# A two-layer spectral and dense kernel: input rows in three parts, three stores from another queue, statistics and residual sums spread

## The chip, the cores and the metric

The kernel runs on one core of one Trainium2 chip. The metric is the device time of one execution in microseconds (us). Before the change it is 927.1 us, the median of three runs (926.85, 927.1 and 933.89). The profiled execution took 925.04 us; its span, from the first to the last instruction, is 923.2 us, with a granted TensorE clock of 1.000. Times with a position, such as 498.55, are us from the start of that span.

## What is computed

`x` is 2048 tokens by 1024 features in bfloat16. A spectral layer and a dense layer alternate twice, each behind a layer norm and with a residual sum:

```python
def _A_ref(x, w_r, w_i):
    X = rfft2(x.astype(f32))                 # 2048 x 513 complex
    return irfft2(X * (w_r + 1j * w_i), s=(S, D)).astype(bf16)
def _B_ref(x, w1, b1, w2):                   # F = 3584
    h = x @ w1 + b1
    return (h * tanh(softplus(h))) @ w2      # Mish
x = x + _A_ref(_layernorm(x)); x = x + _B_ref(_layernorm(x))
x = x + _A_ref(_layernorm(x)); x = x + _B_ref(_layernorm(x))
```

Both layers use the same weights both times. `_layernorm` has no gain and no offset: subtract the row's mean, divide by the root of its variance plus 1e-5.

## The kernel before

All five engines run programs that are written out once, in order. The Python code emits instructions to five lists (`Prog`); a helper (`op`, `group`, `dma`) adds the semaphore waits which the buffers need. So the order on each engine is the order in which the Python code emits, and an instruction that waits holds everything behind it on its engine. The 16 tiles of `x` (128 tokens each) stay in on-chip memory as `XS`; a second copy, `XR`, has the rows laid out for the transforms.

**Spectral layer (`layer_A`).** The two-dimensional transform is a chain of matrix products with tables.
- `s1` (L634): 16 groups j of 8 small matmuls read `XR`. Their results leave PSUM through ScalarE (L640) or VectorE (L642). In the first layer the table `M0` is multiplied by the reciprocal deviation of the rows first (`scaled`, L609 on ScalarE, L615 on VectorE and GpSimd), one 8-block for each j. Three pairs of PSUM banks go round in the first layer, four in the second.
- In the first layer `prologue` loads `XS` and then `XR` from HBM, all on SyncE's queue (L251 is the line of every DMA); `XR` in 24 DMAs of 256-byte rows, for j 0 to 7, 8 to 11 and 12 to 15. A group waits for the whole part that holds it.
- Then, for 8 groups g of frequencies, five kinds of steps, called by digits "stage, g, half": 2 is `s2` (L741), 3 is `s3` (L786 to L789) with the product with the filter on VectorE (L800 to L807), 4 is `i1` (L842), 5 is `i2` (L872, L904). `order_A` is the order of them, written out by hand and used in both layers. Each step takes the next of four PSUM pairs. An `i1` step waits for the filter product of the same g and half. In the first layer `filter_bins` (L1032, with copies on VectorE, L1043, and on ScalarE, L1047) sorts the filter's bins after `s2` of each g.
- The result goes to HBM and back transposed; the last transform (`i4`, L1071) and its exits from PSUM (L573 on ScalarE, L577 on VectorE) run in the dense layer. `spin` and `hold` (L651, L656, L1060) are matmuls with no use but to keep TensorE busy.

**Dense layer (`layer_B`).** Tokens in four chunks c of 512.
- *Opening*: `mm1` (L1220) computes the first hidden features with plain products, in 256-token halves at first, each followed by a Mish on ScalarE (L1224). Three PSUM banks go round, so the matmuls of one group wait for the Mish of the third before. While it runs, the tiles 4 to 7 get their residual sum (`residual`, L1498, VectorE), their statistics, and are normalised (`apply`, L522).
- Statistics of a tile are made by VectorE (`stats_dve`, L470) or by ScalarE (`stats_act`, L451: two passes over the tile, Copy for the sum and Square for the sum of squares). `sums_to_mv` (L462 to L464) and `scales` (L500 to L513), 11 small VectorE operations, turn the sums into a scale.
- *`quads`* (L1260): the other hidden features as 2 by 2 blocks with seven products instead of eight. In each step n VectorE adds partial results from PSUM (L1265), ScalarE applies Mish (L1270) and copies (L573). `after(n)` hangs other work on the step: statistics, residual sums of tiles 12 to 15, `apply`, loads. A product with `A22` reuses a PSUM bank that an L1265 addition must have read.
- *`products`* (L1359): the second matrix product, again with seven block products in place of eight; additions on VectorE (L1398, L1402, L1410).
- At the end of the first dense layer the finished tiles are normalised and stored to `xn_scratch` in HBM (`xn_store`, on GpSimd's queue), and SyncE loads them back as `XR` for the second spectral layer (`xr_load`). The last tile, 11, goes directly from on-chip memory (`xr_direct`, on three queues), while 31 matmuls of `spin` run.

Of the kernel before, what the change touches and what calls it, by code (L numbers as in the profile page):

```python
# [5 lines left out]
ACT = mybir.ActivationFunctionType  # L6
ALU = mybir.AluOpType
P = 128
# [172 lines left out]
class KB:  # L181
# [200 lines left out]
    def prologue(self):  # L382
        sp = self.sp
        self.op(self.pool, lambda e: e.memset(self.EPS[:], 1e-5), writes=[self.r_eps, self.r_warm])
        xt = self.x[0].rearrange("(t p) d -> p t d", p=P)

        for a, b in ((10, 11), (0, 1), (1, 2), (11, 12), (2, 3), (3, 4), (12, 13), (4, 6), (13, 14), (6, 8), (14, 15), (8, 10), (15, 16)):
            self.dma(self.act if a == 10 else sp, self.XS[:, a:b, :], xt[:, a:b, :], f"x{a}", writes=self.r_xs[a:b])
        self.warm(ACT.Sqrt)
        small = {}  # L390
        def load_small(name, n, d):
            b = self.alloc(name, self.o[name], [n], d)
            self.dma(sp, b.ap, self.con[name], name.lower(), writes=[b.res])
            small[name] = b
        load_small("M0", P, BF)
        load_small("IDF", P, F32)
        self.M0, self.IDF = small["M0"], small["IDF"]

        self.XR = self.alloc("XR", self.o["XR"], [P, P])
        self.r_xr = []  # L400
        xv = self.x[0].rearrange("(n2 n1) (h l) -> h n2 n1 l", n2=16, l=P)
        for q, n in ((0, 2), (2, 1), (3, 1)):
            r = Res(f"xr{q}")
            for h in range(8):
                s = slice(32 * q, 32 * (q + n))
                self.dma(sp, self.XR.ap[h:P:8, s, :], xv[h][:, s, :], f"xr{q}", parts=[r])
            self.r_xr += [r] * n
        self.dma(sp, self.FD[:], self.con["FD"], "fd", writes=[self.r_fd])
        load_small("JT", 4 * P, BF)
        self.JT, self.r_jt = small["JT"].ap, small["JT"].res  # L410
        self.w1_next = 0
# [31 lines left out]
                writes=rr)  # L443
        self.op(self.dve, lambda e: e.reciprocal(r, a), writes=rr)

    def stats_act(self, j):
        act = self.act
        x, sums, rs, junk = self.XS[:, j, :], self.BN[:, j, 0:2], self.r_mv[j], self.junk
        rs.begin()
        for i, f in enumerate((ACT.Copy, ACT.Square)):  # L450
            self.op(act, lambda e, i=i, f=f: e.activation(junk.ap, x, f, accum_out=sums[:, i:i + 1]),  # L451
                    reads=[self.r_xs[j]], writes=[junk.res], parts=[rs])

# [70 lines left out]
        return b  # L524


    def xn_store(self, j, b):
        b.unread = False
        self.dma(self.pool, self.xn_d[j].rearrange("h n l -> n h l"), b.ap.rearrange("n (h l) -> n h l", l=P), f"xw{b.res.name[2:]}",
                 reads=[b.res], writes=[self.r_xnd[j]])  # L530

    def open_xr(self):
# [86 lines left out]
    def s1(self, li):  # L619
        self.Y = self.alloc("Y", self.o["Y"], [P, P])  # L620
        self.Y.res.begin()
        M, XR = self.M, self.XR
        for j in range(4 if not li else 0):
            self.scaled(j)
        for j in range(16):
            if not li and self.npair % 4 == 3:

                self.npair += 1
            ps, banks, _ = self.pair()
            fns = []  # L630
            for q in range(8):
                n = 8 * j + q
                m = M[:] if li else self.MN.ap[:, n, :]
                fns.append(lambda e, q=q, n=n, ps=ps, m=m: e.matmul(ps[:, q * P:(q + 1) * P], XR.ap[:, n, :], m,  # L634
                                                                   start=True, stop=True))
            self.group(fns, reads=[self.r_xr[j // 4], self.r_m if li else self.r_mn[j]], writes=banks)
            src = ps.rearrange("p (q k) -> p k q", q=8)
            dst = self.Y.ap[:, :, 8 * j:8 * j + 8]
            if (j % 2 or j == 8) if li else j not in (5, 10, 14):
                self.op(self.act, lambda e, dst=dst, src=src: e.activation(dst, src, ACT.Copy), reads=banks, parts=[self.Y.res])  # L640
            else:
                self.op(self.dve, lambda e, dst=dst, src=src: e.tensor_copy(dst, src), reads=banks, parts=[self.Y.res])  # L642
            if not li and j + 4 < 16:
                self.scaled(j + 4)
        for r in ([self.MN.res, self.M0.res] + self.r_xr if not li else []):
            r.r(self.pe, self.pe.count)
            self.XR.res.r(self.pe, self.pe.count)
# [357 lines left out]
    @staticmethod  # L1005
    def order_A():


        order = ("200 201 210 211 300 301 220 310 400 221 311 401 230 320 410 500 231 321 411 501 330 331 420 510 240 511 421 241 "
                 "250 251 340 341 520 350 430 260 521 431 440 261 351 441 530 531 360 361 270 450 451 271 540 541 550 551 460 370 "  # L1010
                 "461 371 560 561 470 471 570 571")
        return [tuple(map(int, w)) for w in order.split()]
# [144 lines left out]
    def layer_B(self, li, last):  # L1157
        pe, dve, act, sp, pool = self.pe, self.dve, self.act, self.sp, self.pool
# [342 lines left out]
        def turns(c, *ts):  # L1501
            return [lambda t=t: transposed(c, t, xn[4 * c + t]) for t in ts]
# [50 lines left out]
            xn[j] = self.apply(j)  # L1553
        for fg in range(1, 4):
            mm1(0, fg, 1)
            if fg < 3:
                self.stats_act(5 + fg)
        if not last:
            mm1(0, 4)
        at_tiles(1)  # L1560
        B = {"B11": (XT[0].ap[:, 0:4, :], r_xt[0]), "B21": (XT[0].ap[:, 4:8, :], r_xt[0])}
        order = list(early)
        if last:
            block, corner, run = quads(list(range(4, 14)), order, B, [k * 1024 for k in (102, 140)])
            for n, bank in ((0, 3), (1, 4), (2, 5), (3, 0)):
                block(n, bank)
            corner(1, 4)
            turns(1, 0)[0]()
            corner(2, 5)
            turns(1, 1)[0]()  # L1570
            corner(3, 0)
        else:
            mm1(0, 5, mid=turns(1, 0, 1))
# [50 lines left out]
        def after(n):  # L1624
            again = {0: 7, 4: 8, 5: 9} if last else {0: 7}
            if n in again:
                self.fill_slot(order[again[n]], plain + again[n])
            if 1 <= n < 4:
                load_b(STD, n // 3, (n - 1) % 2)
            first = 6 if last else 4  # L1630
            if last:
                if n in (0, 2, 4, 5):
                    self.stats_act(8 + (0, 2, 4, 5).index(n))
                if n == 5:
                    self.xn_buf = self.xn_out + [self.alloc(f"XN{i}", self.ob["XN2"] + i * 2048, [self.D]) for i in range(2)]
                if n in (5, 7):
                    self.sums_to_mv(n + 3, 2)
                    self.scales(n + 3, 2)
            elif n < 4:
                self.stats_dve(8 + n)  # L1640
            elif n == 4:
                self.scales(8, 4)
            if n >= first:
                normal(8 + n - first)
                turn(4)
            for j in {first + 1: (12, 13), first + 2: (14,), first + 3: (15,)}.get(n, ()):
                residual(j)
        run(after, lead)
        self.junk = self.alloc("JUNK2", self.ob["JUNK2"], [self.D])
# [68 lines left out]
        order = [ws[n % 3] for n in range(14)]  # L1718
# [24 lines left out]
        def extra(n, t):  # L1743
            if last:
                return
            if (n, t) == (1, 0):
                PB[6][0] = load_w2("B21", 0, "Q3")
            if (n, t) == (2, 0):
                self.warm(ACT.Sqrt)
            if (n, t) == (3, 3):  # L1750
                self.open_xr()
                for j in range(8):
                    self.xr_load(j)
            if n == 5 and t < 3:
                self.xr_load(12 + t)
            if (n, t) == (5, 2):
                self.xr_load(15)
            if n in (4, 6):
                j = 4 * (n == 4) + 8 + t
                self.stats_second(j, 0, False)  # L1760
                self.root(j, 1)
                b = self.apply(j, out=True)
                if j == 11:
                    self.xr_direct(j, b, 2, (act, pool, sp, pool, sp, act, pool, sp))
                else:
                    self.xn_store(j, b)
            if n == 6 and t < 3:
                if t:
                    self.xr_load(7 + t)
            if (n, t) == (5, 3):  # L1770
                self.xr_load(10)
# [41 lines left out]
```

## Time and profile before

| us from start | stage | length | TensorE busy | VectorE busy | ScalarE busy |
|---|---|---|---|---|---|
| 24 to 42 | first `s1`, start of `s2` | 18 | 15.13 | 12.84 | 15.18 |
| 42 to 60 | first spectral layer, start | 18 | 17.04 | 17.73 | 17.42 |
| 60 to 104 | its rest | 44 | 41.92 | 35.71 | 37.33 |
| 104 to 170 | opening of the first dense layer | 66 | 62.21 | 40.51 | 37.65 |
| 170 to 304 | `quads`, first `products` | 134 | 134.00 | 109.50 | 50.97 |
| 304 to 474 | second half of that layer | 170 | 170.00 | 117.04 | 61.03 |
| 474 to 498 | tile 11, second `s1`, `s2` | 24 | 21.96 | 13.19 | 14.37 |
| 498 to 552 | second spectral layer | 54 | 51.38 | 41.93 | 46.04 |
| 552 to 610 | opening of the second dense layer | 58 | 54.38 | 34.96 | 36.78 |
| 610 to 669 | `quads` | 59 | 58.22 | 40.39 | 37.09 |
| 669 to 751 | `products` | 82 | 82.00 | 51.22 | 12.76 |
| 751 to 923 | second half of that layer | 172 | 168.96 | 91.01 | 50.45 |

Over the span TensorE is busy 877.7 us (95%), VectorE 623.4 (68%), ScalarE 435.0 (47%), GpSimd 147.7 (16%). A row of this table says what an engine did in that stretch, not whether anything waited for it. For that one reads the list of waits (which engine stood still, at which line, and whose instruction ended it), the chain (the path back from the last instruction, each piece with its start and length), and the timeline of one engine in a window, where `[0.62 <-ACT ...]` behind a row is the idle time ahead of it and what ended it. Rows of a timeline are: start, length, engine, line, operation, operands, how many in a row. The end that a matmul row shows lies after the time when the next could have started, because matmuls overlap: in a row of 40 with 256 columns (134.39, 4.53 us) they start about 0.109 us apart, and the last one's shown end is about 0.16 us after the next one's turn.

### The profile page before, as it was taken

How to read it: one execution, taken by the hardware profiler on the slowest of the kernel's cores; microseconds unless marked ns; L12 is line 12 of the kernel's file. 1: busy time of each engine (PE TensorE's matmuls, PEld its weight loads, DVE VectorE, ACT ScalarE, POOL GpSimd, SP SyncE). 2: the span in 40 equal slices, each digit the busy share in tenths (PEclk: the TensorE clock that was granted, in tenths of full speed). 3: DMA queues.
4: the chain of work that ended last, by engine and by line, in shares of the span. 5: the costliest groups of instructions: out<-in, count | busy, mean ns of one | idle time of the engine just before them, and what ended most of it. 6: DMA issues, size and time to landing. Idle time of an engine off the chain costs nothing.

```text
span 923.2 us, 13610 instructions
## 1 busy us (share of the span) xinstructions
PE 877.7 (95%) x5503; PEld 471.1 (51%) x5503; DVE 623.4 (68%) x995; ACT 435.0 (47%) x645; POOL 147.7 (16%) x170
## 2 busy tenths in 40 slices
PE   0899889999999999999998998999999999999998
PEld 0677576444444444444456766754444444444443
DVE  7798468686889667568767765676747655554463
ACT  7898485456203485420018966757540025552000
POOL 0732004960004651010121200000000000000000
PEclk9999999999999999999999999999999999999999
DMA  9979861575786388364723786345166645732432
GB/s 279 284 249 287 219 194 67 210 266 139 262 281 239 131 317 298 121 233 143 281 92 114 221 217 161 137 175 184 23 197 189 204 148 180 269 121 86 173 129 102
DMA packets 153502, 175.98 MB, mean 191 GB/s; under 512 B 75000, under 2 KB 132568, under 8 KB 153320
## 3 DMA queue, kind: packets, MB, share of 16 engines
q1 hardware_dynamic: 140256, 130.32, 45.9%
q0 software_dynamic: 10032, 42.90, 12.5%
q10 hardware_dynamic: 3152, 1.90, 0.7%
q8 instruction: 43, 0.70, 0.3%
q14 instruction: 19, 0.16, 0.0%
HBM read 130.78 MB, written 40.89 MB: 186 GB/s over the span
## 4 chain that ended last, share of the span: by engine, by line
PE 88%; DVE 6%; ACT 3%; SPq 2%; DMA 1%; issue 0%; DVEq 0%
PE PS L1359 37%; PE PS L1260 30%; PE PS L1220 6%; PE PS L741 3%; PE PS L842 2%; PE PS L872 2%; SPq L251 2%; PE PS L1071 2%; PE PS L634 1%; PE PS L651 1%; ACT ARENA L640 1%; PE PS L1181 1%; PE PS L904 1%; PE PS L1060 1%; ACT ARENA L451 1%; PE PS L656 1%
## 5 line engine op out<-in xcount | busy, mean ns | idle before, releaser
L1359 PE MATMUL PS<-ARENA 128*128 128x512 bf16 x1568 | 340.1, 379 | 0.0
L1260 PE MATMUL PS<-ARENA 128*128 128x512 bf16 (+1 forms) x1288 | 280.4, 379 | 0.8 <-DVE ARENA L1265 0.8
L1359 PEld LDWEIGHTS PS<-ARENA 128*128 128x128 bf16 x1568 | 153.3, 98 | 184.5
L1265 DVE TENSOR_TENSOR ARENA<-PS,ARENA 128x512 f32<-128x512 f32 x230 | 157.1, 691 | 100.2 <-PE PS L1260 92.4
L1260 PEld LDWEIGHTS PS<-ARENA 128*128 128x128 bf16 x1288 | 125.3, 98 | 153.3 <-DVE ARENA L1265 3.6
L1270 ACT ACTIVATE ARENA<-ARENA,B 128x512 bf16<-128x512 f32 x138 | 98.8, 721 | 69.1 <-DVE ARENA L1265 63.8
L573 ACT ACTIVATE ARENA<-PS 128x512 f32<-128x512 f32 (+3 forms) x86 | 61.6, 726 | 110.6 <-PE PS L1260 92.5
L1153 POOL TENSOR_TENSOR ARENA<-ARENA 128x512 bf16<-128x512 bf16 x56 | 71.5, 1278 | 74.3 <-DVE ARENA L522 61.1
L451 ACT ACTIVATE ARENA<-XS 128x1024 bf16<-128x1024 bf16 x60 | 63.2, 1053 | 36.6 <-DVE XS L1410 33.0
L1220 PE MATMUL PS<-ARENA 128*128 128x256 bf16 (+1 forms) x528 | 73.4, 295 | 3.4 <-DVE ARENA L1186 1.9
L1384 DVE TENSOR_TENSOR ARENA<-ARENA 128x3584 bf16<-128x3584 bf16 x32 | 63.9, 2017 | 0.0
L1410 DVE TENSOR_TENSOR XS<-PS,ARENA 128x512 bf16<-128x512 f32 x52 | 35.7, 689 | 39.0 <-PE PS L1359 38.7
L1220 PEld LDWEIGHTS PS<-ARENA 128*128 128x128 bf16 x528 | 50.3, 98 | 22.3 <-DVE ARENA L1186 3.3
L1402 DVE TENSOR_TENSOR ARENA<-PS,ARENA 128x512 f32<-128x512 f32 x48 | 32.9, 688 | 28.0 <-PE PS L1359 27.6
L1224 ACT ACTIVATE ARENA<-PS,B 128x256 bf16<-128x256 f32 (+1 forms) x66 | 33.0, 515 | 29.0 <-PE PS L1220 28.8
L1270 ACT ACTIVATE ARENA<-PS,B 128x512 bf16<-128x512 f32 x46 | 31.5, 685 | 18.4 <-PE PS L1260 18.4
L1398 DVE TENSOR_TENSOR ARENA<-ARENA,XS 128x512 f32<-128x512 f32 x52 | 36.8, 731 | 0.5
L442 ACT ACTIVATE RS<-MV,EPS 128x1 f32<-128x1 f32 (+2 forms) x11 | 3.3, 296 | 71.5 <-DVE MV L564 70.1
L741 PE MATMUL PS<-FD,ARENA 128*128 128x256 bf16 (+1 forms) x256 | 31.4, 271 | 2.5 <-ACT ARENA L640 2.5
L842 PE MATMUL PS<-ARENA 128*128 128x256 bf16 x256 | 32.6, 273 | 1.0 <-DVE ARENA L807 0.6
L798 ACT ACTIVATE ARENA<-PS 128x1024 bf16<-128x1024 f32 x30 | 30.4, 1046 | 5.0 <-PE PS L789 5.0
L1235 DVE TENSOR_TENSOR ARENA<-ARENA 128x2048 f16<-128x2048 bf16 x16 | 25.3, 1583 | 9.0 <-PE PS L1220 8.7
(102 smaller groups left out, 811.4 us busy)
## 6 DMA issues: line engine op xcount, KB each, us to landing
ARENA<-in_B_w_dram SPq DMA_DIRECT2D x30, 896.0 KB, 6.7
ARENA<-w1s_scratch SPq DMA_DIRECT2D x28, 896.0 KB, 4.7
ARENA<-w2s_scratch SPq DMA_DIRECT2D x24, 896.0 KB, 6.6
w1s_scratch<-ARENA POOLq DMA_DIRECT2D x14, 896.0 KB, 4.6
ARENA<-in_B_w_dram SPq DMA_DIRECT2D x24, 512.0 KB, 4.3
u_scratch<-ARENA SPq DMA_DIRECT2D x14, 512.0 KB, 4.9
ARENA<-u_scratch SPq DMA_DIRECT2D x14, 512.0 KB, 6.0
w2s_scratch<-ARENA POOLq DMA_DIRECT2D x8, 896.0 KB, 4.1
```

The costliest lines, as they stand in the source:

```text
L451: self.op(act, lambda e, i=i, f=f: e.activation(junk.ap, x, f, accum_out=sums[:, i:i + 1]), reads=[self.r_xs[j]], writes=[junk.res], parts ...
L573: fn = (lambda e: e.activation(dst, src, ACT.Copy)) if scale is None else \
L741: fns.append(lambda e: e.matmul(dst, at(r), FD[:, t:t + n], start=start, stop=stop))
L842: fns.append(lambda e, c=c, part=part: e.matmul(ps[:, c * 256:(c + 1) * 256], yk.ap[:, part, c * P:(c + 1) * P], t[:, (128, 0)[part]:(384, ...
L1153: self.op(self.pool, lambda e, dst=A(dst), x=A(x), y=A(y), op=op: e.tensor_tensor(dst, x, y, op), reads=[b.res] + list(after), writes=[b.rs])
L1220: fns.append(lambda e, db=db, bank=bank, fl=fl: e.matmul(PS[:, bank, 0:w], wb.ap[:, db, fl * P:(fl + 1) * P], x.ap[:, db, tok], start=(db ...
L1260: self.group([lambda e, db=db: e.matmul(PS[:, bank, :], A[:, db, :], mov[:, db, :], start=(start and db == 0), stop=(db == 3), skip_group_ ...
L1265: self.op(dve, lambda e: e.tensor_tensor(dst.ap, PS[:, bank, :], x.ap, ALU.add), reads=[self.r_bank[bank], x.res], writes=[dst.res])
L1270: self.op(act, lambda e: e.activation(at, src, ACT.Mish, bias=self.B1[:, ft:ft + 1]), reads=[res, self.r_b1], writes=[ra])
L1359: self.group([lambda e, i=i, k=k, b=PB[n][k].ap: e.matmul(PS[:, bank, :], ap[:, i, t * P:(t + 1) * P], b[:, i - 7 * k, :], start=(start an ...
L1384: self.op(dve, lambda e: e.tensor_tensor(ap[dst][:, f, :], ap[x][:, f, :], ap[y][:, f, :], op), reads=part(x, k) + part(y, k), writes=part ...
L1398: self.op(dve, lambda e: e.tensor_tensor(a[t], a[t], x, ALU.add), reads=[rx], writes=[r[t]])
```

## The change

Six edits, none of which adds or removes arithmetic.

1. `XR` is loaded for j 0 to 5, 6 to 11 and 12 to 15, so that the first group waits for 48 rows of each 128 in place of 64.
2. `order_A`: step 221 (`s2` of group 2, second half) comes before step 400 (`i1` of group 0) in place of after it.
3. The two ScalarE passes over tile 6 and the two over tile 7 in the opening of the dense layer no longer run as pairs: one pass comes after each of four steps.
4. In the second dense layer the residual sums of tiles 12 and 13 move from `after(7)` to `after(1)` and `after(3)`. Those of tiles 14 and 15 stay, and so do all of the first layer.
5. `xn_store` of tiles 8, 9 and 10 goes through ScalarE's queue; tiles 0 to 7 and 12 to 15 stay on GpSimd's.
6. In the first layer `s1` looks up the part of `XR` by j in place of j // 4, which goes with edit 1.

On the engines this moves: on TensorE 8 matmuls ahead of 8 others, twice; on ScalarE the four passes of each layer, one exit from PSUM ahead of another, twice, and three DMA issues that GpSimd loses; on VectorE two sums; on SyncE 8 of 24 DMAs shrink from 64 to 48 rows and 8 grow from 32 to 48.

```diff
-        for q, n in ((0, 2), (2, 1), (3, 1)):
-            r = Res(f"xr{q}")
+        for j, n in ((0, 6), (6, 6), (12, 4)):
+            r = Res(f"xr{j}")
             for h in range(8):
-                s = slice(32 * q, 32 * (q + n))
-                self.dma(sp, self.XR.ap[h:P:8, s, :], xv[h][:, s, :], f"xr{q}", parts=[r])
+                s = slice(8 * j, 8 * (j + n))
+                self.dma(sp, self.XR.ap[h:P:8, s, :], xv[h][:, s, :], f"xr{j}", parts=[r])
...
-    def stats_act(self, j):
+    def stats_act(self, j, passes=(0, 1)):
...
-        rs.begin()
-        for i, f in enumerate((ACT.Copy, ACT.Square)):
+        if passes[0] == 0:
+            rs.begin()
+        for i in passes:
+            f = (ACT.Copy, ACT.Square)[i]
...
-    def xn_store(self, j, b):
+    def xn_store(self, j, b, prog=None):
...
-        self.dma(self.pool, self.xn_d[j].rearrange("h n l -> n h l"), b.ap.rearrange("n (h l) -> n h l", l=P), f"xw{b.res.name[2:]}",
+        name = f"xv{j}" if prog else f"xw{b.res.name[2:]}"
+        self.dma(prog or self.pool, self.xn_d[j].rearrange("h n l -> n h l"), b.ap.rearrange("n (h l) -> n h l", l=P), name,
...
-            self.group(fns, reads=[self.r_xr[j // 4], self.r_m if li else self.r_mn[j]], writes=banks)
+            self.group(fns, reads=[self.r_xr[j // 4 if li else j], self.r_m if li else self.r_mn[j]], writes=banks)
...
-        order = ("200 201 210 211 300 301 220 310 400 221 311 401 230 320 410 500 231 321 411 501 330 331 420 510 240 511 421 241 "
+        order = ("200 201 210 211 300 301 220 310 221 400 311 401 230 320 410 500 231 321 411 501 330 331 420 510 240 511 421 241 "
...
         for fg in range(1, 4):
             mm1(0, fg, 1)
-            if fg < 3:
-                self.stats_act(5 + fg)
+            self.stats_act(6 + fg // 3, ((fg - 1) % 2,))
         if not last:
             mm1(0, 4)
+            self.stats_act(7, (1,))
...
             corner(1, 4)
+            self.stats_act(7, (1,))
             turns(1, 0)[0]()
...
-            for j in {first + 1: (12, 13), first + 2: (14,), first + 3: (15,)}.get(n, ()):
+            late = {1: (12,), 3: (13,), 8: (14,), 9: (15,)} if last else {5: (12, 13), 6: (14,), 7: (15,)}
+            for j in late.get(n, ()):
                 residual(j)
...
-                    self.xn_store(j, b)
+                    self.xn_store(j, b, act if n == 6 else None)
```

## The prediction

> **What bounds the kernel now.** I read the chain of waits first. By engine:
>
> ```profile
> PE 88%; DVE 6%; ACT 3%; SPq 2%; DMA 1%; issue 0%; DVEq 0%
> ```
>
> The end is set by TensorE. Between 170 and 474 us and between 669 and 751 its busy time equals the length of the stretch, so nothing can be won there; an edit pays only where TensorE stands still. So the list of TensorE's waits came next (us in total, times, longest):
>
> ```profile
> PE PS L634 <- DMA ARENA<-in_A_x_dram: 2.7, 1, 2.7
> ...
> PE PS L1220 <- ACT ARENA L1224: 1.4, 3, 0.6
> ...
> PE PS L1260 <- DVE ARENA L1265: 0.8, 1, 0.8
> ...
> PE PS L842 <- DVE ARENA L807: 0.6, 1, 0.6
> ```
>
> Four of the edits aim at one line each. I then read the timelines around them. A shown idle time is short of the lost time: the last matmul's shown end lies about 0.16 us after the next one's turn. I add 0.16 each time. Opening of the first dense layer, TensorE:
>
> ```profile
> 134.39 4.53 PE L1220 MATMUL PS<-ARENA 128*128 128x256 bf16 x40
> 139.53 2.77 PE L1220 MATMUL PS<-ARENA 128*128 128x256 bf16 x16 [0.62 <-ACT ARENA L1224]
> 142.47 3.63 PE L1220 MATMUL PS<-ARENA 128*128 128x512 bf16 x16 [0.17 <-ACT ARENA L1224]
> ```
>
> ScalarE in the same place:
>
> ```profile
> 136.79 1.06 ACT L451 ACTIVATE ARENA<-XS 128x1024 bf16<-128x1024 bf16 x1
> ...
> 137.97 1.06 ACT L451 ACTIVATE ARENA<-XS 128x1024 bf16<-128x1024 bf16 x1
> ...
> 139.02 0.82 ACT L1224 ACTIVATE ARENA<-PS,B 128x256 bf16<-128x256 f32 x2
> 139.74 1.05 ACT L451 ACTIVATE ARENA<-XS 128x1024 bf16<-128x1024 bf16 x1
> ```
>
> The two passes of tile 6 stand ahead of the Mish that frees a bank; TensorE starts again when it ends. The same picture is at 586.83 (0.61 us idle) in the second dense layer. The first XR part in the chain:
>
> ```profile
> 18.67 5.26 DMA ARENA<-in_A_x_dram
> 23.97 6.14 PE PS L634 x56
> ```
>
> Second spectral layer, step 400 and behind it step 221, which waited for nothing of its own:
>
> ```profile
> 498.55 1.05 PE L842 MATMUL PS<-ARENA 128*128 128x256 bf16 x8 [0.64 <-DVE ARENA L807]
> 499.43 1.04 PE L741 MATMUL PS<-FD,ARENA 128*128 128x256 bf16 x8
> ```
>
> VectorE at step 8 of the second quads (two residual sums, then the additions) and TensorE behind it:
>
> ```profile
> 657.53 1.28 DVE L1498 TENSOR_TENSOR XS<-XS,ARENA 128x1024 bf16<-128x1024 bf16 x2
> 658.74 2.60 DVE L1265 TENSOR_TENSOR ARENA<-PS,ARENA 128x512 f32<-128x512 f32 x4
> ```
>
> ```profile
> 659.48 1.90 PE L1260 MATMUL PS<-ARENA 128*128 128x512 f16 x8 [0.78 <-DVE ARENA L1265]
> ```
>
> **What the Trainium skill says.** "TensorE: Matmul & The Clock Gate", Part 1, gives matmuls of 128 columns 106.7 ns start to start while the array is cold and 55.6 once warm. The trace agrees: in the first s1 they are 107 ns apart from 23.97 to about 29.9 and 55 to 56 after. So the first seven groups cost 0.85 us each. "DMA: Bandwidth & Descriptors", Specifications, wants at least 512 B per transfer for the full rate; the 256 B rows of XR move at 205 to 215 GB/s, the 2 KB rows of XS before them at about 400. So XR is bound by bytes, and a smaller part lands sooner in proportion. The same page, Latency and other measured facts, gives a first byte after about 0.6 us from ScalarE's queue and about 1 from GpSimd's; no row of before shows this store on ScalarE.
>
> **The change part by part.**
>
> *XR in three parts.* The eight DMAs of part one were issued from 7.46 on, the eighth at 18.67, landing 5.26 us later, at 23.93. Six eighths of the bytes are where the sixth was: issued at 16.18, plus the median of 5.2 us, 21.4. But group 0 also needs its scaled table, whose VectorE row (L615) ends at 22.7, and group 1 needs eight ScalarE rows (L609) that end at 24.12. So group 0 starts at 22.75, groups 1 to 5 run from 24.15 at 0.85 us to 28.4, and group 6 now belongs to part two. That part ends with the same byte as before: its last DMA issued at 25.05, plus 3.5, 28.6. Group 6 starts at 28.65 against 29.06: 0.4 us sooner. From there ScalarE's exits (0.92 us each, back to back) keep that, or up to 0.75 if TensorE is warm by then. But at the end of s2's first step stands a fixed time: the filter of group 0 lands for VectorE at 39.24 (L1043, 1.83 us idle for that DMA), and L1032, now at 39.64, cannot come before. The bytes ahead of it are the same. So at most 39.64 - 39.27 = 0.37 us passes. VectorE is then busy almost without a hole to 60 (17.73 of 18.00 us), with its row at 42.04 waiting for TensorE, so the 0.37 carries on. I take 0.35; ends 0 and 0.75 (if the filter lands sooner too).
>
> *Step 221 sooner.* First layer: TensorE waits 0.07 us there, VectorE is the bound and its order is untouched: 0. Second layer: TensorE stands from 497.75 to 498.55, 0.80 us. Step 221 fits in (0.87 us), 400 starts at 498.62 with its operand ready since 498.49, and 311 starts at 499.47 against 500.30: 0.83. VectorE's products then hold back 401 (ready at 500.49) and ScalarE's exit of 320 comes 0.6 sooner (its exits are 0.91 us apart and three stand ahead of it), so 0.6 is what survives. From there to 543.7 TensorE has no hole, so it arrives at the end. Ends 0.3 and 0.83. What is queued behind the moved exit on ScalarE is 400's, 0.3 us later than before; its reader, step 500, comes at 504.65, far off.
>
> *Statistics spread.* A pass costs 1.15 us on ScalarE, as in the pair at 136.79 and 137.97. First dense layer: with one pass at a time the Mish of TensorE's third group back ends at about 138.4, ahead of 138.76, when its bank is wanted; the next two slabs have ScalarE at 2.1 us a pair against TensorE's 1.75, a deficit of 0.35 us each that the three banks absorb. Both waits go: 0.62 + 0.16 + 0.17 + 0.16 = 1.1 us. Tile 7's sums are complete at 145.1 in place of 142.1; VectorE asks for them at about 146.8: free. Second: 0.61 + 0.16 = 0.77; the last pass then stands behind the first corner's Mish, ends near 593.2, and VectorE's sums are wanted at 593.9. Together 1.9; ends 1.1 (new small waits) and 1.9.
>
> *Residual sums of 12 and 13.* Without them the addition at 658.74 starts at 657.6 and ends at 658.3, and the product that reuses its bank has its turn at 658.54: the whole 0.78 + 0.16 = 0.94 us goes. At after(1) and after(3) each sum (0.61 us) falls in a hole: VectorE's rows at 622.38, 626.79 and 632.84 have idle times of 1.03, 1.03 and 1.63 us ahead of them. Ends 0.7 and 0.95.
>
> *Stores from ScalarE.* ScalarE does nothing between its root rows at 463.83, 466.86, 469.88 and 475.99, so an issue of under 1 us waits for nobody and nobody for it; GpSimd loses three rows of 0.89 us. The next spectral layer begins at 481.09, after tile 11, whose DMAs are issued from 477.09, and after 31 filler matmuls; tiles 8 to 10 are not last. 0; ends -0.2 (their packets next to other loads) and +0.2.
>
> Sum: 0.35 + 0.6 + 1.9 + 0.94 + 0 = 3.8 us. All five shifts stand on the chain one after the other, and the matmuls between them are back to back, so they add. 927.1 - 3.8 = 923.3.
>
> **The rivals.**
> 1. *The spectral edits vanish*: the filter's DMA or group 6's wait takes all of the first, ScalarE's exits all of the second. For it: ScalarE is busy 17.42 of 18.00 us in 42 to 60 and 46.04 of 54 in 498 to 552. Against: at 499.63 it had just waited 0.51 us for step 400. 1.9 + 0.94 = 2.8: 924.3.
> 2. *Spread passes make new waits*: ScalarE is slower than TensorE over four slabs by up to 4 x 0.35 = 1.4 us, twice. Against: three banks, and no Mish that frees a bank has two passes ahead of it any more. Half the statistics' gain and rival 1 together: 0.95 + 0.94 = 1.9: 925.2.
> 3. *Slower*: part two of XR lands later than 28.6, so that the array starts cold, stops and warms late; and the loads ahead of tile 11 come to lie on its own, so that the second s1 starts after the fillers have ended. Each such wait is of the size of those seen here (2.7 us for the first): some 1.5 us more than before, 928.6. Against: the bytes and their order on SyncE's queue are the same.
>
> **How the numbers follow.** Forecast 0.65, first rival 0.17, second 0.12, third 0.06. The best ends add up to 0.75 + 0.83 + 1.9 + 0.95 + 0.2 = 4.6, so 922.5; less 1.0 for the difference between executions (half of the 2.06 us between the profiled one, 925.04, and the median) gives 921.5 as the low end. The high end takes in the second rival and the same allowance: 926.2. Outside it lie the third rival and little more. One per cent is 9.3 us, twice the best sum, so faster by that is 0.02, slower 0.03, the same 0.95.
>
> **What would show it.** In the profile after: the first L634 at 22.75 and the group waiting for the second part near 28.6; no L1220 wait for L1224 in either opening; L741 in place of the hole at 497.75; no L1260 wait for L1265; the second s1 as long after its fillers as now. It would be wrong if TensorE's summed waits fell by much less than 3.5 us, or if holes came up in the stretches that are full now.

## The result

The changed kernel takes 925.8 us in the median of 22 executions, the kernel before, run beside it, 927.6. The ratio on record is 0.9971, 95% interval 0.9961 to 0.9981. That is 2.7 us (0.0029 x 927.6) of the 3.8 that were forecast. It is not the quotient of the two medians, which is 0.9981 (1.8 us); that of the two means is 0.9973. All prices below go by the ratios on record. The time lies in the range 921.5 to 926.2, nearer to the second rival's 925.2 than to the forecast's 923.3.

### The profile page after: what moved, and what is told of

The parts are those of the page before. It is cut to its first block, busy times and chain, and to the rows that moved or that the text cites. A ratio compares the mean times of both kernels' runs of the same rounds, so it can differ in the third digit from the quotient of the medians.

```text
span 924.8 us, 13610 instructions
## 1 busy us (share of the span) xinstructions
PE 879.3 (95%) x5503; PEld 473.1 (51%) x5503; DVE 623.3 (67%) x995; ACT 434.8 (47%) x645; POOL 145.5 (16%) x167
## 4 chain that ended last, share of the span: by engine, by line
PE 88%; DVE 5%; SPq 3%; DMA 2%; ACT 2%; issue 0%; DVEq 0%
PE PS L1362 35%; PE PS L1263 30%; PE PS L1223 7%; PE PS L744 3%; SPq L251 3%; PE PS L845 2%; PE PS L875 2%; PE PS L1074 2%; ACT ARENA L643 1%; PE PS L1184 1%; PE PS L907 1%; PE PS L1063 1%; PE PS L659 1%; PE PS L637 1%; DMA xn_scratch<-ARENA 1%; PE PS L789 1%
## 5 line engine op out<-in xcount | busy, mean ns | idle before, releaser
L1263 PE MATMUL PS<-ARENA 128*128 128x512 bf16 (+1 forms) x1288 | 280.2, 379 | 0.0
L1268 DVE TENSOR_TENSOR ARENA<-PS,ARENA 128x512 f32<-128x512 f32 x230 | 157.1, 690 | 99.2 <-PE PS L1263 91.5
L1263 PEld LDWEIGHTS PS<-ARENA 128*128 128x128 bf16 x1288 | 125.6, 98 | 152.0 <-DVE ARENA L1268 2.1
L1156 POOL TENSOR_TENSOR ARENA<-ARENA 128x512 bf16<-128x512 bf16 x56 | 71.3, 1273 | 73.6 <-DVE ARENA L524 59.9
L1223 PE MATMUL PS<-ARENA 128*128 128x256 bf16 (+1 forms) x528 | 72.9, 295 | 2.0 <-DVE ARENA L1189 1.9
L1223 PEld LDWEIGHTS PS<-ARENA 128*128 128x128 bf16 x528 | 50.4, 98 | 20.2 <-DVE ARENA L1189 3.3
L1227 ACT ACTIVATE ARENA<-PS,B 128x256 bf16<-128x256 f32 (+1 forms) x66 | 33.2, 515 | 28.0 <-PE PS L1223 27.8
L744 PE MATMUL PS<-FD,ARENA 128*128 128x256 bf16 (+1 forms) x256 | 32.9, 279 | 2.5 <-ACT ARENA L643 2.5
L845 PE MATMUL PS<-ARENA 128*128 128x256 bf16 x256 | 32.7, 273 | 0.3
```

Of the source, the lines that this page charges most:

```text
L744: fns.append(lambda e: e.matmul(dst, at(r), FD[:, t:t + n], start=start, stop=stop))
L845: fns.append(lambda e, c=c, part=part: e.matmul(ps[:, c * 256:(c + 1) * 256], yk.ap[:, part, c * P:(c + 1) * P], t[:, (128, 0)[part]:(384, ...
L1156: self.op(self.pool, lambda e, dst=A(dst), x=A(x), y=A(y), op=op: e.tensor_tensor(dst, x, y, op), reads=[b.res] + list(after), writes=[b.rs])
L1223: fns.append(lambda e, db=db, bank=bank, fl=fl: e.matmul(PS[:, bank, 0:w], wb.ap[:, db, fl * P:(fl + 1) * P], x.ap[:, db, tok], start=(db ...
L1263: self.group([lambda e, db=db: e.matmul(PS[:, bank, :], A[:, db, :], mov[:, db, :], start=(start and db == 0), stop=(db == 3), skip_group_ ...
L1268: self.op(dve, lambda e: e.tensor_tensor(dst.ap, PS[:, bank, :], x.ap, ALU.add), reads=[self.r_bank[bank], x.res], writes=[dst.res])
```

## The profile after

The chain of waits by engine, from the page of the changed kernel:

```profile
PE 88%; DVE 5%; SPq 3%; DMA 2%; ACT 2%; issue 0%; DVEq 0%
```

TensorE still sets the end; SyncE's queue and transfers have one point each more. Line numbers lie 3 higher than before around TensorE's lines (L634 is now L637, L1220 L1223, L1260 L1263). From TensorE's list of waits (total, times, longest):

```profile
PE PS L637 <- DMA ARENA<-ARENA: 2.9, 1, 2.9
...
PE PS L637 <- DMA ARENA<-in_A_x_dram: 1.1, 1, 1.1
```

The first line wasn't in the list before. `ARENA<-ARENA` is tile 11's own rows, copied from on-chip memory to `XR`: the second `s1` waits for them. The second line is the new second part of `XR`. The waits that answer to the three other lines aimed at (L1223 for L1227, L1263 for L1268, L845 for VectorE) are gone.

*Opening of the first dense layer.* TensorE's timeline, then ScalarE's:

```profile
135.60 10.58 PE L1223 MATMUL PS<-ARENA 128*128 128x256 bf16 x72
```

```profile
138.00 1.06 ACT L453 ACTIVATE ARENA<-XS 128x1024 bf16<-128x1024 bf16 x1
...
139.06 0.82 ACT L1227 ACTIVATE ARENA<-PS,B 128x256 bf16<-128x256 f32 x2
139.77 1.05 ACT L453 ACTIVATE ARENA<-XS 128x1024 bf16<-128x1024 bf16 x1
...
140.81 0.83 ACT L1227 ACTIVATE ARENA<-PS,B 128x256 bf16<-128x256 f32 x2
```

One pass, two halves of a Mish, one pass: the 72 matmuls run in one piece of 10.58 us. Before, the same 72 took from 134.39 to 146.10 (142.47 + 3.63), 11.71 us. Gain 1.13.

*Second spectral layer*, TensorE, where it stood still at 497.75 before:

```profile
502.07 1.04 PE L744 MATMUL PS<-FD,ARENA 128*128 128x256 bf16 x8
502.94 1.04 PE L845 MATMUL PS<-ARENA 128*128 128x256 bf16 x8
```

Step 221 (L744) fills the hole, and step 400 (L845) follows without a wait.

*Step 8 of the second quads*, VectorE, then TensorE:

```profile
659.99 0.54 DVE L524 TENSOR_SCALAR FD<-XS,MV,RS 128x1024 bf16<-128x1024 bf16 x1
660.45 2.76 DVE L1268 TENSOR_TENSOR ARENA<-PS,ARENA 128x512 f32<-128x512 f32 x4
```

```profile
656.70 9.23 PE L1263 MATMUL PS<-ARENA 128*128 128x512 bf16 x42
```

The residual sums no longer stand ahead of the additions, and TensorE has no hole where it lost 0.78 us.

*Opening.* The first `s1` and `s2` on TensorE, and from the chain the last DMA of `XR`'s second part:

```profile
22.69 1.01 PE L637 MATMUL PS<-ARENA 128*128 128x128 bf16 x8 [1.68 <-DVE ARENA L618]
23.95 4.16 PE L637 MATMUL PS<-ARENA 128*128 128x128 bf16 x40 [0.25 <-ACT ARENA L612]
29.23 1.51 PE L637 MATMUL PS<-ARENA 128*128 128x128 bf16 x24 [1.12 <-DMA ARENA<-in_A_x_dram]
...
37.86 3.14 PE L744 MATMUL PS<-FD,ARENA 128*128 128x256 bf16 x16 [1.16 <-ACT ARENA L643]
```

```profile
24.63 4.55 DMA ARENA<-in_A_x_dram
```

Group 0 starts at 22.69, 1.28 us sooner. Group 6 then waits for this part, whose last DMA took 4.55 us to land. `s2` starts at 37.86 against 38.11 before, and its first 16 matmuls take 3.14 us, where they took 1.69 before.

*Tile 11 and the second `s1`*. Before, the chain ran over TensorE, from the filler matmuls (L651) to the second `s1` (L634) with 0.21 us between them:

```profile
474.19 6.69 PE PS L651 x31
480.88 0.21 issue
481.09 0.62 PE PS L634 x8
```

After, from 471 us on:

```profile
471.37 5.72 DMA xn_scratch<-ARENA
...
477.10 0.63 SPq L251
...
479.06 4.75 DMA ARENA<-ARENA
...
484.16 4.48 PE PS L637 x48
```

This is where the missing part went, as the experiments show. The chain now runs over the third moved store, tile 10's, which takes 5.72 us. SyncE's load of tile 10 waits for it (477.10), stands ahead of tile 11's rows on the queue, and moves beside them; the rows take 4.75 us, and TensorE, whose fillers ended at 481.26, starts at 484.16. Two stretches of the same profile (length, then busy time of TensorE, its weight loads, VectorE, ScalarE and GpSimd, then granted clock, DMA share and GB/s):

```profile
37.90:41.30 3.40, 3.40 (x19) 2.52 (x20) 1.37 (x2) 1.29 (x2) 3.40 (x5) 0.50 1.05 384
...
485.00:488.50 3.50, 3.50 (x37) 3.50 (x35) 2.91 (x3) 2.05 (x2) 0.00 (x0) 0.51 0.00 0
```

Soon after each of the two stops, the one of 1.16 us ahead of `s2` and the one of 2.90 us, TensorE runs at half clock for 3.4 us. The second `s1` takes 9.65 us from first to last matmul for 8.39 before.

## The experiments

Three theories stood at first.

- A: the stores from ScalarE's queue give a part back, at tile 11.
- B: `XR` in three parts gives it back, at the opening.
- C: nothing is given back, and the profiled execution was an unlucky one.

All ratios are to the kernel before on the same chip; 0.001 is 0.93 us. The two columns on the right come from one trace of each kernel (e7's is the slowest of its executions).

| kernel | ratio | 95% interval | TensorE's wait for tile 11, us | load of tile 10 issued ahead of tile 11's first rows by, us |
|---|---|---|---|---|
| before | 1 | | 0.21, no DMA | 2.59 |
| changed | 0.9971 | 0.9961 to 0.9981 | 2.90 | 0.38 |
| e1, stores only | 1.0020 | 1.0007 to 1.0033 | 2.70 | 0.53 |
| e2, `XR` only | 0.9988 | 0.9974 to 1.0002 | 1.33 | 2.33 |
| e3, statistics and sums only | 0.9975 | 0.9962 to 0.9988 | 1.56 | 2.30 |
| e4, all but the stores | 0.9952 | 0.9934 to 0.9970 | 1.29 | 2.34 |
| e5, all but stores and `XR` | 0.9959 | 0.9946 to 0.9972 | 0.67 | 2.57 |
| e6, store of tile 10 only | 0.9993 | 0.9980 to 1.0005 | 1.04 | 2.37 |
| e7, stores of tiles 8 and 9 only | 1.0020 | 1.0008 to 1.0031 | 2.60 | 0.40 |
| e8, `XR` in four parts only | 1.0044 | 1.0026 to 1.0061 | 0.22, no DMA | 2.51 |
| e9, all, but of the stores only tile 10's | 0.9957 | 0.9943 to 0.9970 | 0.37 | 2.38 |
| e10, as e9 without `XR` | 0.9970 | 0.9957 to 0.9983 | 0.54 | 2.45 |
| e11, all but `XR` | 0.9988 | 0.9976 to 1.0000 | 2.39 | 0.54 |
| e12, order only | 0.9991 | 0.9974 to 1.0007 | 1.10 | 2.40 |

### Which part gives it back: e1 to e4

e1 has this edit alone, and e4 lacks it:

```diff
-                    self.xn_store(j, b)
+                    self.xn_store(j, b, act if n == 6 else None)
```

> Only the edit of xn_store: tiles 8 to 10 are stored from ScalarE's queue. Theory A (the gains came as computed, and this store gives part of them back, because it lands late, so that tile 10's rows are loaded while tile 11's are): slower than before by 0.8 to 2 us, ratio 1.001 to 1.002, and in the profile the second s1 starts after its fillers with TensorE waiting for the DMA of tile 11 (2.9 us in the profile of the changed kernel). Theory B (XR in three parts gives it back): ratio 1.000. Theory C (nothing is given back, the profiled execution of the changed kernel was an unlucky one): ratio 1.000 and no wait.

> The whole change without the stores from ScalarE. Theory A: 3.5 to 3.8 us faster than before, ratio 0.996, and 0.8 to 2 us faster than the changed kernel; the second s1 begins right after its fillers, as before. Theory B: 2.3 to 2.7 us faster, ratio 0.9972, as the changed kernel. Theory C: 3.8 us faster, ratio 0.996, and the changed kernel the same in the long run.

e1 is slower than before by 1.9 us, its interval clear of one, with about the wait of the changed kernel (2.70 us). e4, the mirror of it, is 4.5 us faster than before, where 3.5 to 3.8 were expected; it rests on six executions, with an interval from 2.8 to 6.1. Its second `s1` was to begin right after its fillers and began 1.29 us after them, so this expectation missed. Theory A holds; C, by which nothing is given back, falls with e1. e2 has this edit and the lookup that goes with it, e3 the passes and the sums:

```diff
-        for q, n in ((0, 2), (2, 1), (3, 1)):
+        for j, n in ((0, 6), (6, 6), (12, 4)):
```

> Only XR in three parts. Theory A: first L634 group near 22.7, second part landed at 28.6 to 29.2, at most 0.35 us gained: ratio 0.9996 to 1.000. Theory B (a stop between the parts leaves the array cold in the first s2, whose 16 matmuls took 3.14 us in place of 1.69): slower by about 1.2 us, ratio 1.0013. Theory C: 0.35 us faster, 0.9996.

```diff
-            if fg < 3:
-                self.stats_act(5 + fg)
+            self.stats_act(6 + fg // 3, ((fg - 1) % 2,))
...
-            for j in {first + 1: (12, 13), first + 2: (14,), first + 3: (15,)}.get(n, ()):
+            late = {1: (12,), 3: (13,), 8: (14,), 9: (15,)} if last else {5: (12, 13), 6: (14,), 7: (15,)}
```

> Only the spread statistics and the moved residual sums. All theories: 1.9 + 0.94 = 2.8 us faster, ratio 0.997, and no wait of L1220 for L1224 or of L1260 for L1265 in the profile. Less than 2 us would say that these gains are smaller than the sum over their waits, and that theories A and B look for a loss that is none.

e3 gains 2.3 us; the steps had 1.9 + 0.94 = 2.8, well inside its interval, and neither of the waits aimed at is in its trace. e2 is at 0.9988, and its interval allows a cost of 0.2 us at most, so B falls.

### What it is about the stores: e5 to e7

Two readings of A were left. A1: tile 9's sooner store releases the load of tile 9, which lies on tile 10's store. A2: a store in 256-byte pieces from ScalarE's queue is slow in itself. e6 moves tile 10 alone, e7 tiles 8 and 9 without it; e5 is the change without the stores and without `XR`.

```diff
-                    self.xn_store(j, b)
+                    self.xn_store(j, b, act if j == 10 else None)
```

is e6, and e7 is

```diff
-                    self.xn_store(j, b)
+                    self.xn_store(j, b, act if n == 6 and j < 10 else None)
```

> Order, statistics and sums without XR in three parts and without the ScalarE stores. If the three parts gain nothing (theory: TensorE starts 1.3 us sooner but then stops 1.1 to 1.9 us for the second part and drops to half clock for 3.4 us), this is as fast as the change without the stores: 0.6 + 1.9 + 0.94 = 3.4 us faster than before, ratio 0.9963. If the three parts gain their 0.35 us, it is 0.35 slower than that, which is below what can be measured; if they cost, it is faster, up to 4.5 us under before.

> Only tile 10 is stored from ScalarE's queue; 8 and 9 stay on GpSimd's; everything else as before. Theory A1 (tile 10's store is late in the changed kernel because tile 9's store, landing 2.6 us sooner, releases the load of tile 9 on top of it): here tile 10's store lands 2.3 to 2.9 us after its issue, the second s1 waits 1.3 us or less and the array stays warm there; time 1.000 or a little under. Theory A2 (a store of 256-byte packets from ScalarE's queue is slow by itself): it lands over 5 us after its issue, the second s1 waits some 2.7 us, ratio 1.002.

> Tiles 8 and 9 are stored from ScalarE's queue, tile 10 from GpSimd's, everything else as before. Theory A1: tile 10's store is as late as in the changed kernel (4.5 us or more after its issue), since the load of tile 9 starts at the same time as there; the second s1 waits over 2 us; ratio 1.001 to 1.002. Theory A2: it lands 2.9 us after its issue as before, the wait is 1.3 us or less, ratio 1.000.

e5 is 3.8 us faster than before, where 3.4 were expected. e6 costs nothing (0.9993), e7 costs all of it (1.0020), though its slow store is GpSimd's. In e6 tile 10's store took 3.57 us, between the 2.3 to 2.9 of A1 and the 5 and more of A2: from ScalarE's queue a store is slower by itself, but by about 0.7 us (3.5 to 3.6 in e6, e9 and e10, against 2.8 to 2.9 for the same tile in the seven traces that store all three from GpSimd's queue). The stores in e7, from the view of the tensor `xn_scratch` (count, ns that the issue holds the queue, first and last start), and its chain:

```profile
L251 ACTq DMA_DIRECT2D xn_scratch<-ARENA x2: 372/378/383, 468.6 to 471.6; - x2
L251 POOL DMA_DIRECT2D xn_scratch<-ARENA x1: 887/887/887, 475.0 to 475.0; - x1
...
DMA to landing us min/median/max: 2.3/3.9/5.3
```

```profile
475.04 5.27 DMA xn_scratch<-ARENA
```

The slowest of the three, 5.27 us, is tile 10's, the one on the old queue; the fastest, 2.3, is one of ScalarE's. So A2 falls as the cause of the loss, and what matters is what runs beside a store. SyncE's queue shows it. In the changed kernel, for a window that begins ahead of the load of tile 8:

```profile
469.53 1.76 SPq L251 DMA_DIRECT2D ARENA<-xn_scratch  x2
```

and in the kernel before, for a window from 472 on:

```profile
473.32 1.82 SPq L251 DMA_DIRECT2D ARENA<-xn_scratch  x2
```

After, tiles 8 and 9 are loaded back in one burst between 469.53 and 471.29, and tile 10's store starts at 471.37, on top of it. Before, that store (2.8 us, the shortest of its three) was issued at 471.65, after tile 8's load and ahead of tile 9's at 473.32. Before, then, the slow store was tile 9's (4.8 us, the longest), beside tile 8's load, and it put off tile 9's load until it harmed nobody. The table's last column separates the cases without an exception: in the four traces in which tile 9 is stored from ScalarE, tile 10's load goes out 0.4 to 0.5 us ahead of tile 11's rows and TensorE waits 2.4 to 2.9 us; in the ten others it goes out 2.3 to 2.6 us ahead and TensorE waits 0.2 to 1.6. The mean wait is 2.65 us in the four and 0.83 in the ten. The difference, 1.8 us, is near the price of e1 and e7; the 0.21 of the one trace of before is at the low end of the ten. No run moved tile 8's store or tile 9's alone, and none held tile 9's load back with the stores as they are: that e7's two stores cost is shown, the step by way of tile 9's load is read from the traces.

A part of this price is the clock. Each execution's record has its mean granted clock, and one stretch of 3.41 us at half clock lowers it by 0.0018 (3.41 x 0.5 / 925). It is 0.998 or lower in 67 of the 88 executions of the four kernels that store tile 9 from ScalarE, in 85 of 173 of the kernel before and in 69 of 137 of the other versions without e8. So half clock is more frequent with these stores, and in three of the four traces (not e11's) a stretch of it begins within 1 us of the stop's end.

"DMA: Bandwidth & Descriptors", Queues, rings and completion order, of the Trainium skill states that each DMA engine goes round the queues which have work for it and takes one whole packet from each. In the changed kernel's trace the packets of tile 8's and 9's loads are 32 KB and take 1.8 us each, those of the stores from ScalarE's queue 256 bytes and 18 ns. That agrees with a store being held up by loads beside it, and with 5.3 and 5.7 us against 2.3; no run changed the packet size, so the cause of the slow store is only argued.

### Other sizes of the first parts: e8

To see whether the stop ahead of `XR`'s second part can be avoided, groups 6 and 7 got a part of their own, and the rest was loaded in two:

```diff
-        for q, n in ((0, 2), (2, 1), (3, 1)):
+        for j, n in ((0, 6), (6, 2), (8, 4), (12, 4)):
```

> Only XR, in four parts: groups 0 to 5, 6 and 7, 8 to 11, 12 to 15. TensorE starts as early as with three parts (22.7) but groups 6 and 7 wait for no more bytes than before, so the stop of 1.1 to 1.9 us goes. If that stop is what eats the edit's gain: no wait over 0.5 us for XR after the first, no drop of the clock in the first s1 and s2, s1 ends 0.7 us sooner than before, and 0.4 us or more arrives (ratio 0.9995 or less). If the gain is limited elsewhere: 1.000.

Both expectations missed, a gain of 0.4 us or none: it cost 4.1 us. Its first `s1` on TensorE:

```profile
28.88 0.61 PE L634 MATMUL PS<-ARENA 128*128 128x128 bf16 x8 [0.18 <-ACT ARENA L640]
31.06 3.28 PE L634 MATMUL PS<-ARENA 128*128 128x128 bf16 x32 [1.57 <-DMA ARENA<-in_A_x_dram]
37.51 2.94 PE L634 MATMUL PS<-ARENA 128*128 128x128 bf16 x32 [3.17 <-DMA ARENA<-in_A_x_dram]
```

and the chain, at one of the DMAs of 16 rows:

```profile
19.98 0.61 SPq L251
```

A DMA of 16 rows holds SyncE's queue for 0.61 us, one of 32 rows 0.63 and one of 48 rows in the changed kernel about 0.85. So the 32 DMAs are issued over 25.6 us (7.70 to 33.29), where the 24 of before take 23.0 (7.46 to 30.42), and TensorE stands 3.17 us for the last part. At this size the issue sets the pace; the prediction held `XR` to be bound by its bytes. Half clock adds to it: in this trace TensorE has it for 3.41 us from 31.44 and for 6.83 us from 38.26, and the mean granted clock of all nine executions is 0.993 to 0.996.

### The pieces put together again: e9 to e12

e9 is the changed kernel but for one condition:

```diff
-                    self.xn_store(j, b, act if n == 6 else None)
+                    self.xn_store(j, b, act if j == 10 else None)
```

> The changed kernel, but tiles 8 and 9 are stored from GpSimd's queue as before and only tile 10 from ScalarE's. Theory A1 (what costs is that tile 9's sooner store releases the load of tile 9 onto tile 10's store, which then holds back the load of tile 10 and tile 11's rows): tile 10's store alone has no load behind it that could lie on it, so this is the changed kernel without its loss: about 4.5 us below the kernel before, as the version without the store edit, some 924.2 us; TensorE's wait for tile 11's rows at the second s1 stays under 1.5 us. Rival (any store on ScalarE's queue in that stretch costs): the wait is 2.5 us or more and the time about 926.

e9 is at 0.9957, 4.0 us below before, where 4.5 was expected. TensorE waits 0.37 us for tile 11. The chain:

```profile
476.38 0.54 SPq L251
...
477.59 2.60 DMA ARENA<-ARENA
...
480.54 0.62 PE PS L637 x8
```

Tile 11's rows now go out when the tile is ready and take 2.60 us in place of 4.75. e9 (923.9 us) and e4 (923.95) are the fastest versions, 1.3 and 1.8 us below the changed kernel by ratio; the intervals overlap with its.

e10 is e9, and e11 the changed kernel, with `XR` loaded and looked up as before:

```diff
-        for j, n in ((0, 6), (6, 6), (12, 4)):
+        for q, n in ((0, 2), (2, 1), (3, 1)):
...
-            self.group(fns, reads=[self.r_xr[j // 4 if li else j], self.r_m if li else self.r_mn[j]], writes=banks)
+            self.group(fns, reads=[self.r_xr[j // 4], self.r_m if li else self.r_mn[j]], writes=banks)
```

> Order, statistics and residual sums changed, tile 10 stored from ScalarE, XR in the parts of before. Theory: XR in three parts is worth nothing, since the stop before its second part takes back the sooner start: within 0.6 us of the same kernel with XR in three parts, about 924.5 us. The prediction's price of the XR part: 0.35 us more than it. Rival (XR in three parts costs, by the half-clock stretch that a stop can bring): about 1 us less than it.

> The changed kernel with XR in the parts of before, so order, statistics, residual sums and all three stores from ScalarE. If the stores alone give back the missing part (about 1.7 us) and XR nothing: 924.8 + 1.7 = 926.5 us, 2.2 below the kernel before, and TensorE waits 2.5 us or more for tile 11's rows at the second s1. If XR in three parts gives back most of it: about 925, as without the stores.

The idea that `XR` in three parts is worth nothing, which e2's trace had suggested, does not fit well: e10 is 1.2 us slower than e9, where at most 0.6 was expected, and e11 is 1.1 us below before, where 2.2 were expected, and 1.6 slower than the changed kernel. But such a difference is uncertain by about 1.5 to 1.8 us, so neither run settles it. e11 also has the stores' wait, 2.39 us.

e12 has the order alone:

```diff
-        order = ("200 201 210 211 300 301 220 310 400 221 311 401 230 320 410 500 231 321 411 501 330 331 420 510 240 511 421 241 "
+        order = ("200 201 210 211 300 301 220 310 221 400 311 401 230 320 410 500 231 321 411 501 330 331 420 510 240 511 421 241 "
```

> Only step 221 ahead of step 400. The prediction's price: 0.6 us, from the second spectral layer alone: ratio 0.9993, about 928.1 us, and TensorE's stretch from the second s2 to the third spin-up 59.9 us in place of 60.5. The rival that spectral edits vanish: 0, that stretch 60.5 us.

0.9991, with an interval that holds 0 and 1.5 us alike. The traces say more: from the second `s2` to the third spin-up TensorE takes 60.53 us before (491.00 to 551.53) and 59.91 in the changed kernel (495.33 to 555.24), 0.62 less. It is 59.9 in all seven traces that have the new order and 60.5 in the seven others. (e9 to e12 read 60.13 or 60.14: the spin-up's first matmul, 0.22 us, has no record in these traces.)

## Why the prediction was right, and where it failed

With the table each part has several prices, alone and as a difference of two kernels. A single one is uncertain by 1.1 to 1.7 us, a difference by 1.5 to 2.1, and prices that share a kernel are not independent:

| part | prices, us | mean | forecast |
|---|---|---|---|
| `XR` in three parts | e2 -1.1, e4 less e5 -0.6, e9 less e10 -1.2, changed less e11 -1.6 | -1.1 | -0.35 |
| order | e12 -0.8, e5 less e3 -1.5 | -1.2 | -0.6 |
| statistics and residual sums | e3 -2.3, e5 less e12 -3.0 | -2.6 | -2.84 |
| stores of tiles 8, 9 and 10 | e1 +1.9, changed less e4 +1.8, e11 less e5 +2.7 | +2.1 | 0 |
| sum | | -2.8 | -3.8 |

- *Statistics spread*: right in cause and size. 1.13 us in the first dense layer for 1.1. In the second, the 48 matmuls that took 6.20 us with their stop (581.68 to 587.88) take 5.40: 0.80 for 0.77.
- *Residual sums*: right. From the third spin-up to TensorE's last matmul 368.43 us before and 366.69 after, 1.74 less; without the 0.80 above, 0.94 remains, as forecast.
- *Step 221 sooner*: right in the trace, 0.62 for 0.6; the times can't tell 0.6 from 1.2.
- *XR in three parts*: group 0 at 22.69 for 22.75, right. The second part was to land at 28.6 (25.05 + 3.5) and landed at 29.18 (24.63 + 4.55): the median landing of the old, smaller DMAs was too short for it. So group 6 starts at 29.23, later than the 29.06 of before, and this part of rival 3 came true. Against that, e9's first L1035 runs at 39.04, ahead of the 39.27 that the step held for the earliest: the filter's landing is no fixed floor. The four prices agree in sign, mean 1.1, and leave room for 0.35. Leaving out e8, `s2` starts no more than 0.1 us sooner on average with three parts than with the old ones (38.35 in four traces against 38.43 in nine, with a scatter of 0.8 and 0.5), so where 1.1 would come from stays open.
- *Stores from ScalarE*: this step failed. It read "0; ends -0.2 (their packets next to other loads) and +0.2", because the next spectral layer begins after tile 11 and "tiles 8 to 10 are not last". They aren't last, but they share the DMA engines and SyncE's queue with the last. A store that lands 2.6 us sooner (tile 9's, 470.67 in place of 473.30) is no gain when nobody waits for it, and it released a load at the wrong time. The price is +2.1 us in place of at most +0.2: the longer wait and, after it, half clock in more executions. The sign "the second s1 as long after its fillers as now" showed it: 2.90 us in place of 0.21.
- *The rivals*: rival 3 had named this wait ("the loads ahead of tile 11 come to lie on its own") and dismissed it with "the bytes and their order on SyncE's queue are the same". The order was the same and the times weren't. It ended faster than before because the other parts brought more than it cost. Rivals 1 and 2 came near in time by chance. Of rival 1's waits group 6's appeared (1.12 us), but the order's gain stayed; of rival 2's none did.

So the total fell short by 1.1 us. The stores cost about twice that, and the four other parts together brought about 4.9 us for the 3.8 forecast. That this surplus made up for half of the failed step is luck, and it is why the total came near. (The table's sum meets the measured 2.7 partly by construction, since the changed kernel stands in two of the prices.)

## What to carry to other kernels

A transfer that is sooner than anyone needs isn't free: ask what its completion releases, and what that will run beside. On a queue in order, follow the last transfer that matters back to everything queued ahead of it, with times, not only with the order. And price an edit that should cost nothing by running it alone, since gains elsewhere hide it.

## What the runs showed of the hardware

- The stores of tiles 8 to 10, 256 KB each, took 2.3 to 4.2 us, but 4.8 to 5.7 where a load to `XR` had been issued within 1.1 us ahead of them or 0.2 us behind them, on either queue and once in each of the 14 traces. Apart from such a load, tile 8's took 3.9 to 4.2 us from ScalarE's queue and 3.2 to 3.4 from GpSimd's, so the small pieces may cost something of their own. And tile 11's pieces of 16 KB took up to 2.8 us to land in e9 and up to 4.8 in the changed kernel, where the load of tile 10 was issued 0.4 us ahead of them in place of 2.4.
- A stretch of 3.41 us at half clock costs 1.3 to 1.5 us (9.65 - 8.39, 3.14 - 1.69), half of this change's gain. So a single profile doesn't rank versions: that of the changed kernel, with two such stretches, has a span of 924.8 us, 1.6 longer than that of before, which has none.
- Whether a stop of TensorE brings half clock depends on where it falls. "TensorE: Matmul & The Clock Gate", Part 1, of the Trainium skill tells of a free-running window of about 3.4 us and that the result varies from run to run. The traces agree: in each of the 14 all changes of the granted clock lie whole multiples of 3.41 us apart (10.24, 443.73 and 436.91 us in the changed kernel: 3, 130 and 128 times). If the traces are cut at these multiples, half clock followed each of the 11 full-clock windows in which TensorE was busy for 1.62 us or less, 5 of 16 between that and 1.80 us, and none of 3614 with more; some matmul records are missing, which blurs the middle group. The stop of 2.90 us in the changed kernel left 0.89 us of work in its window; that of 2.39 us in e11 lay across a border, left 1.68, and brought none. No stop ahead of a half-clock stretch was as long as a whole window: two stops of 0.9 us in one window, as in e5 at 568, were enough.
